# q's 32 x 32 squares: put in place by copies, or by way of memory

## The chip, the cores and the metric

The kernel runs on one core of a Trainium2 chip. Its engines, as the profile names them: PE (TensorE, matmuls), DVE (VectorE), ACT (ScalarE), POOL (GpSimd) and SP (SyncE, which here only issues DMAs). Each engine works through its own queue of instructions in order; an instruction that waits holds up what stands behind it on its engine. The metric is the time of one execution in microseconds, as the device measures it.

## The reference

Linear attention with two softmaxes, and then a mixer of two layers over tokens and two over channels, in fp32, for 8 batches, 8 heads, 576 positions and 64 numbers per head:

```python
q_s = softmax(q, axis=-1)             # over the 64 numbers of a head
k_s = softmax(k, axis=2)              # over the 576 positions
kv  = einsum('bhsd,bhse->bhde', k_s, v)
att = einsum('bhsd,bhde->bhse', q_s, kv)
x   = att.transpose(0, 2, 1, 3).reshape(8, 576, 512)
h   = maximum(x.transpose(0, 2, 1) @ w_tok1, 0) @ w_tok2
u   = x + h.transpose(0, 2, 1)
out = u + maximum(u @ w_ch1, 0) @ w_ch2
```

## The kernel before

Attention and the token mixer are cut into 32 units, numbered 0 to 31: one batch and two heads each (128 channels). A unit loads k (twice, as it is and turned), q and v, makes the two softmaxes, and then goes through five stages on PE: `stage_qT` and `stage_kv`, `stage_y` (q times w_tok1), `stage_h1`, and `stage_u` in two halves, which adds q times kv and the token mixer's second layer. The results are the columns of u. The channel mixer takes u in nine groups of 512 columns; its steps (`ch1` or `pair_a`/`pair_b`, and `ch2`) are the bulk of PE's work, and the stages of the units are spread between these steps.

Every number that goes into a matmul of a late unit (8 to 31) is split into two parts of reduced precision, a high one made by ACT (a copy that rounds, `nc.scalar.copy`) and a low one, the difference, made by DVE or POOL. `split` does both; its instructions carry the lines L134 and L135.

`stage_qT` of a late unit has to turn q: 128 positions by 128 channels, five such tiles, of which the last one holds 64 positions. DVE's transpose (L395) turns each square of 32 x 32 in its place: what it writes to the tile `cv_s` has the right numbers in each square, but a square that belongs to the partitions of group x and the columns of group y still stands at partitions y, columns x. Sixteen copies (L405), one for each pair of groups, carry the squares across partitions back into q's own tile `q_t`, which is free again once `qh` (ACT) and `ql` (POOL) have been made of it. Units 8 to 11 give every second copy to DVE and ACT; from unit 12 on DVE has 6 and ACT 10 of the 16. Then `qth` (ACT, L134) and `qtl` (DVE, L135) are made of the turned q. They are read by `stage_u` (L461), and once they are made, the load of q of the unit after next may overwrite `q_t`, of which there are two buffers (L165, issued by SP).

SP also issues the loads of `kt_t`, `k_t` and `v_t` (L173, L178, L187), the stores and loads of weights that are made on the way (L504 to L547), and, from group 3 on, the loads of the channel mixer's weights into `ring` (L585), eight buffers that PE (L642) empties in turn. The order of all instructions on each engine is fixed when the program is built, by a scheduler that places them by its own estimate of their times; the tables of steps in the code set only where a stage may begin.

The calls of `stage_qT` are in `pe_stages` (its first stage); the first late unit (8) reaches it about 167 us into the execution, the last (31) at about 642 us.

## Time and profile before

| what | value |
|---|---|
| median of 3 runs | 805.53 us (805.46 to 806.17) |
| profiled execution | 804.5 us, of which the span of its instructions is 802.7 us |
| granted TensorE clock | 1.0 |
| PE busy | 770.3 us (96%) |
| DVE busy | 654.6 us (82%) |
| ACT busy | 409.7 us (51%) |
| POOL busy | 180.2 us (22%) |
| DMA | 159.10 MB, mean 198 GB/s |

The span is what the profile's rows cover; the 1.8 us beside it lie before and after the first and the last instruction. PE's matmuls overlap each other, so that a matmul's own duration (0.39 us for 512 columns) is longer than the distance from one to the next (0.23 us). In rows of the timeline, the first number is the start in us from the span's start and the second the time that the row covers; a row of several instructions of one kind is one row with x and a count, and it may cover short waits between them; in brackets stands how long the engine was idle before it and who ended this wait. Rows with SPq or ACTq are issues of DMAs.

### The profile page before, as it was taken

To read this page: it belongs to the slowest core of one execution; us is meant where nothing else is said; L and a number is where in the kernel's file an instruction comes from. 1 tells how busy PE (TensorE), PEld (TensorE's weight loads), DVE (VectorE), ACT (ScalarE), POOL (GpSimd) and SP (SyncE) were. 2 spreads that over 40 slices of the span, in tenths; PEclk is the share of its full clock that TensorE was granted. 3 is DMA by queue.
4 is the path that set the end of the run, shared out by engine and by line. 5 is a ranking of instruction groups with operands and counts; after the bars stand their busy time and mean duration, and the time that the engine had idled before them with its cause. 6 is when DMAs were issued, how large, how long until landed. Compare 5 with 4: busy or idle time off the path is not lost.

```text
span 802.7 us, 13549 instructions
## 1 busy us (share of the span) xinstructions
PE 770.3 (96%) x4824; PEld 669.0 (83%) x4824; DVE 654.6 (82%) x1229; ACT 409.7 (51%) x952; POOL 180.2 (22%) x130
## 2 busy tenths in 40 slices
PE   3899999989999999999999999979999999999998
PEld 2688888877887888899999999869888998888886
DVE  7989998899879787987798679898998557567971
ACT  4776533465654565555564455555654534246610
POOL 0000000101211244122212121232512320446640
PEclk9999999999999999999999999999999999999999
DMA  9754842325777675575667666798956443666675
GB/s 305 218 151 150 297 148 93 110 64 186 232 240 264 220 234 162 182 256 179 188 205 228 197 179 204 252 309 246 292 166 208 142 135 110 193 195 192 194 206 197
DMA packets 124963, 159.10 MB, mean 198 GB/s; under 512 B 49376, under 2 KB 71520, under 8 KB 124896
## 3 DMA queue, kind: packets, MB, share of 16 engines
q1 hardware_dynamic: 118560, 145.91, 58.7%
q10 hardware_dynamic: 6336, 12.32, 4.1%
q8 instruction: 38, 0.62, 0.3%
q14 instruction: 29, 0.24, 0.1%
HBM read 123.60 MB, written 34.60 MB: 197 GB/s over the span
## 4 chain that ended last, share of the span: by engine, by line
PE 59%; DVE 22%; issue 7%; DMA 7%; ACT 3%; POOL 1%; SPq 0%; DVEq 0%; POOLq 0%; ACTq 0%
PE ps_o L691 16%; PE ps_h L642 10%; PE ps_h L765 7%; PE ps_o L765 6%; PE ps_h L461 6%; DMA q_t<-in_q 4%; PE ps_h L484 4%; PE ps_h L419 4%; DVE q_t L405 2%; PE ps_h L357 2%; DVE q_t L327 1%; DVE st L337 1%; DVE st L326 1%; DVE st L338 1%; PE ps_o L461 1%
## 5 line engine op out<-in xcount | busy, mean ns | idle before, releaser
L691 PE MATMUL ps_o<-h,c2h 128*128 128x512 f32 x544 | 182.4, 397 | 2.5 <-ACT h L487 2.5
L691 PEld LDWEIGHTS ps_o<-h,c2h 128*128 128x128 f32 x544 | 101.3, 188 | 22.6 <-ACT h L487 3.4
L691 PE MATMUL ps_o<-h,c2l 128*128 128x512 f32 x272 | 105.8, 392 | 0.0
L318 POOL TENSOR_TENSOR k_t<-k_t,dg 128x640 f32<-128x640 f32 x24 | 40.4, 1683 | 202.5 <-ACT dg L317 177.5
L135 POOL TENSOR_TENSOR ql<-q_t,qh 128x640 fp32r<-128x640 f32 x24 | 40.1, 1669 | 177.5 <-PE ps_o L691 101.0
L405 ACT COPY q_t<-cv_s 32x160 f32<-32x160 f32 (+1 forms) x232 | 71.8, 310 | 3.0 <-DVE cv_s L395 0.2
L642 PE MATMUL ps_h<-th,ring 128*128 128x256 f32 x384 | 71.7, 283 | 1.2 <-DVE c L673 1.2
L642 PEld LDWEIGHTS ps_h<-th,ring 128*128 128x128 f32 x384 | 59.9, 191 | 1.6 <-DVE c L673 1.6
L691 PEld LDWEIGHTS ps_o<-h,c2l 128*128 128x128 f32 x272 | 51.2, 188 | 8.7
L642 PE MATMUL ps_h<-uh,ring 128*128 128x256 f32 x288 | 54.8, 283 | 2.0 <-DVE c L669 2.0
L484 PE MATMUL ps_h<-uh,c1l 128*128 128x512 f32 x144 | 56.2, 391 | 0.0
L484 PE MATMUL ps_h<-ul,c1h 128*128 128x512 f32 x144 | 56.2, 390 | 0.0
L484 PE MATMUL ps_h<-uh,c1h 128*128 128x512 f32 x144 | 56.1, 392 | 0.0
L642 PE MATMUL ps_h<-tl,ring 128*128 128x256 f32 x192 | 54.3, 283 | 0.0
L336 ACT ACTIVATE q_t<-q_t 128x640 f32<-128x640 f32 x32 | 23.6, 738 | 51.7 <-DVE q_t L327 41.2
L642 PEld LDWEIGHTS ps_h<-uh,ring 128*128 128x128 f32 x288 | 46.0, 190 | 4.1 <-DVE c L669 2.2
L468 ACT CAST uh<-ps_h 128x320 fp32r<-128x320 f32 (+4 forms) x76 | 24.5, 335 | 46.1 <-PE ps_h L461 30.5
L326 DVE TENSOR_REDUCE st<-q_t 128x10 f32<-128x640 f32 x32 | 26.2, 817 | 24.2 <-DMA q_t<-in_q 24.1
L405 DVE COPY q_t<-cv_s 32x160 f32<-32x160 f32 (+1 forms) x152 | 37.8, 249 | 4.1 <-POOL ql L135 2.3
L642 PE MATMUL ps_h<-ul,ring 128*128 128x256 f32 x144 | 40.6, 282 | 0.0
L469 DVE TENSOR_TENSOR ul<-ps_h,uh 128x320 fp32r<-128x320 f32 (+4 forms) x76 | 27.2, 369 | 13.1 <-ACT uh L468 12.8
L642 PEld LDWEIGHTS ps_h<-tl,ring 128*128 128x128 f32 x192 | 36.8, 191 | 0.0
(321 smaller groups left out, 2110.4 us busy)
## 6 DMA issues: line engine op xcount, KB each, us to landing
ring<-w SPq DMA_DIRECT2D x210, 256.0 KB, 3.5
ring<-v SPq DMA_DIRECT2D x42, 256.0 KB, 3.0
kt_t<-in_kt SPq DMA_DIRECT2D x32, 320.0 KB, 3.7
q_t<-in_q SPq DMA_DIRECT2D x32, 320.0 KB, 3.7
v_t<-in_v SPq DMA_DIRECT2D x32, 320.0 KB, 4.3
stg_w<-in_w SPq DMA_DIRECT2D x18, 512.0 KB, 6.1
k_t<-in_k SPq DMA_DIRECT2D x24, 320.0 KB, 5.0
w<-stg SPq DMA_DIRECT2D x12, 512.0 KB, 4.2
```

The source lines that it names most:

```text
L135: lo_eng.tensor_tensor(lo, src, f32(hi), op=ALU.subtract)
L318: nc.gpsimd.tensor_tensor(kx, kx, dg.unsqueeze(1).broadcast_to([P, C1, P]), op=ALU.subtract)
L326: nc.vector.tensor_reduce(st[:, 0, :], qt, axis=AX.X, op=ALU.max)
L405: eng(qx[ys, 0:n, xs], turned[xs, 0:n, ys])
L419: nc.tensor.matmul(y[:, 0:TOK], a, w, start=(i == 0), stop=(i == len(mm) - 1))
L461: nc.tensor.matmul(t[:, 0:N], a, w, start=(i == 0), stop=(i == len(mm) - 1))
L468: nc.scalar.copy(uh, src).ins,
L469: nc.vector.tensor_tensor(ul, src, f32(uh), op=ALU.subtract).ins,
L484: nc.tensor.matmul(t, a[:, n, :], w, start=(i == 0), stop=(i == 3 * NJ - 1))
L642: nc.tensor.matmul(t[:, cols], a, b[:, n], start=(i == 0), stop=(i == 5))
L691: m = nc.tensor.matmul(o, a[:, cs], w, start=(first and i == 0), stop=(last and i == 2))
L765: nc.tensor.matmul(o, a, b, start=first and i == 0 and (n == 0 or not one), stop=last and i == 2 and (n == 1 or not one))
```

## The change

The sixteen copies are gone. The transpose writes its squares in another order within a partition (first by the group of columns, then by tile), so that the four parts of a partition, 5 x 32 numbers (640 bytes) each, can be stored by one DMA into a buffer in memory, `q8` to `q31`, one for each unit (L397, issued by SP). Four more DMAs (L399, SP too), one for each group of 32 partitions, load them to their new partitions, again 640 bytes at a time, into `q_t`. There they stand in an order of their own, and `qth` and `qtl` are made by two splits instead of one, of 512 and of 64 columns, that read `q_t` through a view with four axes and write the same `qth` and `qtl` as before.

```diff
@@ stage_qT, late units @@
-        turned = cv.tile([P, C1 * P], U32, name="cv_s").bitcast(F32).rearrange("p (c t) -> p c t", t=P)
-        nc.vector.transpose(turned, qx)
-        k = 0
-        for x in range(P // Q):
-            n = C1 if x * Q < TL else C
-            for y in range(P // Q):
-                xs, ys = slice(x * Q, (x + 1) * Q), slice(y * Q, (y + 1) * Q)
-
-                both = (nc.vector.tensor_copy, nc.scalar.copy)
-                eng = both[k % 2] if u["n"] < NE + NJ else both[k % 3 > 0]
-                k += 1
-                eng(qx[ys, 0:n, xs], turned[xs, 0:n, ys])
-        split(qth, qtl, qx.rearrange("p c t -> p (c t)")[:, 0:S], nc.vector)
+        turned = cv.tile([P, C1 * P], U32, name="cv_s").bitcast(F32).rearrange("p (y c t) -> p y c t", y=P // Q, t=Q)
+        nc.vector.transpose(turned.rearrange("p y c t -> p c y t"), qx.rearrange("p c (y t) -> p c y t", t=Q))
+        dq = dpool.tile([P // Q, P, C1 * Q], F32, name=f"q{u['n']}")
+        nc.sync.dma_start(dq.rearrange("y p f -> p y f"), turned.rearrange("p y c t -> p y (c t)"))
+        for y in range(P // Q):
+            nc.sync.dma_start(
+                qx[y * Q : (y + 1) * Q].rearrange("r c t -> r (c t)").rearrange("r (x f) -> r x f", x=P // Q),
+                dq[y].rearrange("(x r) f -> r x f", r=Q),
+            )
+        back = qx.rearrange("p c t -> p (c t)").rearrange("p (x c t) -> p c x t", x=P // Q, t=Q)
+        for hi, lo, src in ((qth[:, 0:S0], qtl[:, 0:S0], back[:, 0:C]), (qth[:, S0:S], qtl[:, S0:S], back[:, C, 0 : TL // Q, :])):
+            if len(src.shape) == 4:
+                hi, lo = (x.rearrange("p (c x t) -> p c x t", c=C, t=Q) for x in (hi, lo))
+            else:
+                hi, lo = (x.rearrange("p (x t) -> p x t", t=Q) for x in (hi, lo))
+            split(hi, lo, src, nc.vector)
```

Because the scheduler works out its order anew, other instructions move too. Line numbers behind the change are 3 higher (L461 becomes L464, L484 L487, L585 L588, L691 L694).

On **ACT**, at unit 13 (`qh` L347 is the last piece of qh, `hh` L434 is unit 13's hidden layer that `stage_u` takes, `h` L487 a step of the channel mixer). Before:

```order
L347 CAST qh<-ql 64x128
L487 ACTIVATE h_129<-ps_h 128x512
L405 COPY q_t<-cv_s 32x5x32 x5
L405 COPY q_t<-cv_s 32x4x32 x5
L434 ACTIVATE hh<-ps_h 128x256
L487 ACTIVATE h_129<-ps_h 128x512
```

And now:

```order
L347 CAST qh<-ql 64x128
L490 ACTIVATE h_129<-ps_h 128x512
L437 ACTIVATE hh<-ps_h 128x256
L134 CAST stg<-stg 128x1024
L490 ACTIVATE h_129<-ps_h 128x512
L134 CAST qth<-q_t 128x512
L134 CAST qth<-q_t 128x64
```

The ten copies that stood ahead of `hh` are gone, and `qth`, in two pieces, stands four rows behind `hh`.

On **PE**, at unit 8, the first late unit (L427 is its `stage_h1`, L461 with `qth` its `stage_u`, L484 and L691 are the channel mixer's two layers). Before:

```order
L427 MATMUL ps_h<-kvf_98,ys 128x128 x2
L461 MATMUL ps_h<-qth,kvh 128x320
L484 MATMUL ps_h<-uh_123,c1h_115 128x512
L484 MATMUL ps_h<-uh_123,c1l_116 128x512
L484 MATMUL ps_h<-ul_124,c1h_115 128x512
...
L691 MATMUL ps_o<-h_129,c2h_1258 128x512
L691 MATMUL ps_o<-h_129,c2l_1259 128x512
```

And now:

```order
L430 MATMUL ps_h<-kvf_98,ys 128x128 x2
L694 MATMUL ps_o<-h_129,c2h_1258 128x512
L694 MATMUL ps_o<-h_129,c2l_1259 128x512
...
L694 MATMUL ps_o<-h_129,c2h_1258 128x512 x4
L464 MATMUL ps_h<-qth,kvh 128x320
L487 MATMUL ps_h<-uh_123,c1h_115 128x512
L487 MATMUL ps_h<-uh_123,c1l_116 128x512
```

The twelve matmuls of L691, which came behind the twelve of L484, now stand ahead of the first one that reads `qth`.

On **SP**, where unit 17's squares come back (group 3 of the channel mixer; the names end in numbers of buffers; `q_3531` is unit 17's buffer in memory and `q_3770` unit 18's). Before:

```order
L173 DMA kt_t<-in_kt 128x640
L585 DMA ring_3167<-w_2162 128x512
L585 DMA ring_3168<-w_2162 128x512
L585 DMA ring_3169<-w_2162 128x512
L585 DMA ring_3170<-w_2162 128x512
L585 DMA ring_3171<-w_2162 128x512
```

And now:

```order
L173 DMA kt_t<-in_kt 128x640
L588 DMA ring_3103<-w_2138 128x512
L588 DMA ring_3104<-w_2138 128x512
L397 DMA q_3770<-cv_s 128x4x160
L588 DMA ring_3105<-w_2138 128x512
L588 DMA ring_3106<-w_2138 128x512
L399 DMA q_t<-q_3531 32x4x160 x4
L588 DMA ring_3107<-w_2138 128x512
```

The store of unit 18 and the four loads of unit 17 stand between loads of the ring; the ring's next load waits behind the four.

## The prediction

> **What bounds the kernel now.** I read the busy time of the engines in stretches of 50 us first, and then who made PE wait while late units are in work, 160 to 650 us.
>
> ```profile
> 150.00:200.00 50.00, 45.62 (x280) 38.07 (x279) 45.64 (x96) 27.42 (x68) 6.36 (x4) 1.00 0.42 132
> 400.00:450.00 50.00, 50.00 (x362) 46.05 (x362) 40.50 (x83) 27.30 (x71) 8.31 (x6) 1.00 0.66 206
> 500.00:550.00 50.00, 45.81 (x328) 40.80 (x327) 42.28 (x83) 25.75 (x66) 14.08 (x7) 1.00 0.84 271
> ```
>
> Each row has the stretch and its length, then the busy time of PE, PEld, DVE, ACT and POOL, the granted clock, DMA's share and GB/s. PE sets the time: 50.00 of 50 us at 400. What a faster DVE or ACT can give is what PE lacks elsewhere, in stretches in which DVE is busier than there (45.64 and 42.28 against 40.50). The waits name it:
>
> ```profile
> PE ps_o L691 <- ACT h L487: 2.5, 2, 1.3
> PE ps_h L642 <- DVE c L669: 2.0, 1, 2.0
> PE ps_h L461 <- ACT qth L134: 1.8, 1, 1.8
> PE ps_h L461 <- ACT hh L434: 1.3, 2, 0.9
> PE ps_h L642 <- DVE c L673: 1.2, 1, 1.2
> PE ps_h L461 <- DVE hl L435: 1.0, 2, 0.7
> PE ps_o L691 <- DVE h3l L679: 0.8, 1, 0.8
> PE ps_h L461 <- ACT kvh L134: 0.7, 1, 0.7
> ```
>
> Total, count and longest, in us. The eight make 11.3 us; what is left out is smaller. So the change can't give much more than 11 us, 1.4% of the time, whatever it takes off DVE and ACT.
>
> **What is removed.**
>
> ```profile
> L405 DVE COPY q_t<-cv_s x152: 205/225/1687, 169.1 to 644.0; 32x160 f32<-32x160 f32 x76, 32x128 f32<-32x128 f32 x76
> ```
> ```profile
> L405 ACT COPY q_t<-cv_s 32x160 f32<-32x160 f32 (+1 forms) x232 | 71.8, 310 | 3.0 <-DVE cv_s L395 0.2
> L405 DVE COPY q_t<-cv_s 32x160 f32<-32x160 f32 (+1 forms) x152 | 37.8, 249 | 4.1 <-POOL ql L135 2.3
> ```
>
> ACT loses 71.8 us and DVE 37.8: from unit 12 on, ten copies of 0.31 us on ACT and six of 0.25 on DVE per unit. Most of that is hidden behind PE. It counts where PE waited for something queued behind copies:
>
> ```profile
> 246.65 3.20 ACT L405 COPY q_t<-cv_s 32x160 f32<-32x160 f32 x10
> 249.88 0.38 ACT L434 ACTIVATE hh<-ps_h 128x256 fp32r<-128x256 f32 x1
> 600.41 3.20 ACT L405 COPY q_t<-cv_s 32x160 f32<-32x160 f32 x10
> 603.63 0.30 ACT L134 CAST kvh<-kvf 128x128 fp32r<-128x128 f32 x1
> ```
> ```profile
> 579.86 2.46 DVE L405 COPY q_t<-cv_s 32x160 f32<-32x160 f32 x6
> 582.35 0.69 DVE L679 SCALAR_TENSOR_TENSOR h3l<-c,h3h 128x512 fp32r<-128x512 f32 x1
> ```
> ```profile
> 535.66 1.00 DVE L405 COPY q_t<-cv_s 32x160 f32<-32x160 f32 x4
> 536.69 0.42 DVE L435 SCALAR_TENSOR_TENSOR hl<-ps_h,hh 128x256 fp32r<-128x256 f32 x1
> ```
>
> `hh`, `kvh`, `h3l` and `hl` each start right behind copies, and each is in the list of waits. Term A: 1.3 (both waits for hh) + 0.7 (kvh) + 0.8 (h3l) + 0.7 (the longer for hl) = 3.5 us gained; 0 if other work takes the copies' place, 3.5 at most.
>
> **What is added on ACT and DVE.** One split of 576 columns becomes two, of 512 and 64.
>
> ```profile
> L468 ACT CAST uh<-ps_h 128x64 fp32r<-128x64 f32 x14 | 3.0, 213 | 11.2 <-PE ps_h L461 10.1 <-DVE ul L469 1.0
> 169.97 0.62 ACT L134 CAST c2h<-cv_s 128x512 fp32r<-128x512 f32 x1
> 341.36 0.67 ACT L134 CAST qth<-q_t 128x576 fp32r<-128x576 f32 x1
> ```
>
> 0.62 + 0.21 for 0.67 us: 0.16 more on ACT per unit, and as much on DVE, 24 x 0.16 = 4 us each, a tenth of what DVE loses. It goes with the copies it replaces: hidden, and if not hidden 0.16 a unit. No row shows a read through this four-axis view or a transpose that writes in this order; I take the same times.
>
> **The way through memory.** The store and loads move 2 x 24 x 327,680 bytes = 15.7 MB on top of 159.10. Durations from the nearest rows (issue to landing, 150 to 300 us):
>
> ```profile
> w<-stg SPq DMA_DIRECT2D x12, 512.0 KB, 4.2
> q_t<-in_q SPq DMA_DIRECT2D x7, 320.0 KB, 4.4
> w<-c1h SPq DMA_DIRECT2D x6, 128.0 KB, 5.0
> v<-c2h SPq DMA_DIRECT2D x2, 128.0 KB, 3.5
> out<-part ACTq DMA_DIRECT2D x4, 256.0 KB, 2.1
> 182.66 0.47 SPq L505 DMA_DIRECT2D w<-c1h  x1
> ```
>
> A store of 320 KB: 4.2 us by the nearest. A load of 80 KB: between 2.1 and 5.0, I take 3.5, the nearer small one. Four issues are 0.5 us apart, so the last begins 1.5 after the first.
>
> In the steady part this is covered. Unit 17, as an example:
>
> ```profile
> 333.02 1.57 POOL L135 TENSOR_TENSOR ql<-q_t,qh 128x640 fp32r<-128x640 f32 x1 [3.75 <-ACT qh L134]
> 355.71 0.36 PE L461 MATMUL ps_h<-qth,kvh 128*128 128x256 f32 x1
> ```
>
> The loads may start when ql is made, 334.6; the store only needs the transpose, long done. 334.6 + 1.5 + 3.5 = 339.6, before the 341.36 at which ACT takes up qth (row above), and PE reads it 14 us later. Cost 0. On SP the four issues delay the ring's next load by 2 us; a ring buffer is refilled when PE has emptied it, and used again seven or more products later:
>
> ```profile
> ring<-w SPq DMA_DIRECT2D x210, 256.0 KB, 3.5
> L642 PE MATMUL ps_h<-th,ring x384: 278/283/386, 332.1 to 677.4; 128*128 128x256 f32 x192
> ```
>
> PE does 168 products (24 pairs of steps, seven each) in these 345 us: they take 2.05 us each, so seven are 14 us, less 3.5 for the load: 10 us of cover. Cost 0; it begins when SP is held for 10.
>
> At unit 8 it is not covered: there PE waited for `qth` already.
>
> ```profile
> 163.28 3.12 DMA whole<-cv_s
> 166.50 0.85 DVE L395 STREAM_TRANSPOSE cv_s<-q_t 128x640 f32<-128x640 f32 x1 [0.52 <-DMA whole<-cv_s]
> 171.86 0.42 PE L461 MATMUL ps_h<-qth,kvh 128*128 128x320 f32 x1 [1.84 <-ACT qth L134]
> 206.62 2.77 PE ps_o L691 x12
> ```
>
> The transpose ends at 167.35; a store of 256 KB at this place took 3.1, and with the loads (1.5 + 3.5) and the first cast (0.62) qth is there at 176.1. PE could go on at 170.0 (171.86 - 1.84) and now first does the twelve matmuls moved ahead, 2.8 us, to 172.8. It then waits 3.3 where it waited 1.8. Term B: 1.5 us lost; with 3.1 and 2.1 it is 0.1, with 4.4 and 5.0 it is 4.3.
>
> The Trainium skill (DMA: Bandwidth & Descriptors, Anatomy of one DMA) has about 2.0 us fixed plus bytes at 436 GB/s, fitted there for the other way of issuing. An estimate by it is 2.75 us for the store and 2.2 for a load, B would be about -0.1, and the forecast 1.6 lower. This trace is slower than that rule at 128 KB (3.5 and 5.0), so I stay with the rows.
>
> **Term C, the waits that are not behind a copy.** L487's 2.5 and L669's and L673's 3.2 sit in the stretches at 150 and 500. DVE loses 37.8 - 4 = 34 us of the some 480 us in which late units run, 7%, and the order is new, so these waits may vanish or come back elsewhere: -5.7 to +5.7. I take a fifth, -1.1. Ahead of L669's wait DVE took 2.02 us for ten numbers per partition, so more than the amount of work decides there:
>
> ```profile
> 526.76 2.02 DVE L338 TENSOR_SCALAR st<-st 128x10 f32<-128x10 f32 x1
> ```
>
> **Sum.** -3.5 + 1.5 - 1.1 = -3.1 us on the profiled execution's own 804.5, of which 802.7 are the span. That execution is 1.0 below the median of the runs; from the median, 805.53 - 3.1 = 802.4 us.
>
> The Trainium skill (SBUF — State Buffer, section SBUF: two separate sides) says that DVE and POOL share one pair of ports as an exclusive lock, and that a DVE instruction with two inputs from SBUF, or in a two-port mode as copies can be, waits for the whole POOL instruction. The one long copy (1687 ns against a median of 225) and the 2.02 us agree. By it A would gain at most 1.5 us more, since fewer of DVE's instructions can be caught; one copy of 152 was, so the sum leaves it out.
>
> **The rivals.** *Slower, by loads that land late.* `qth` now waits in ACT's queue for DMAs, and `qtl` in DVE's for `qth`. Behind `qth` on ACT stand the copies of u and the hidden layer `h` (L678), for which DVE's low part and then PE's L691 wait; behind the four loads on SP stands the ring. The cover at unit 17 is 341.36 - 339.6 = 1.8 us, so this decides once the last load takes over 3.5 + 1.8 = 5.3 us. For it: DMA's share is 0.84 at 500 (0.66 at 400), the slowest 128 KB row is already 5.0, and SP's order can hold the loads back. Price: at 6.0 us ACT stands 0.7 us longer in each of, say, 12 units (half of them), 8.4 us, and without cover on PE that is 805.5 - 3.1 + 8.4 = 810.8 us. Against it: median landings of 3.5 to 4.4 and PE's 14 us until it reads `qth`.
>
> The Trainium skill (DMA: Bandwidth & Descriptors, same section) holds most of the fixed time to be the wait for the write's receipt, longest when the target is memory, and that speaks for this rival, since each unit now writes memory and waits for it. Here 512 KB to memory (`w<-stg`) landed in 4.2 us and 320 KB from it (`q_t`) in 4.4: no surcharge is seen.
>
> *No change.* PE was bound before and stays so; A comes back as waits elsewhere, since freed queues only reach the next wait sooner, and B cancels the rest: 805.5 us. For it speaks 50.00 of 50 us at 400; against it that four named waits are directly behind copies.
>
> *More than forecast.* DVE's relief empties the full stretches: A 3.5, C 5.7, B 0.1 lost: 9.1 us, 796.4 us. Against it: nothing in C names a copy.
>
> **Chances.** The forecast (802.4) has 0.40, late loads 0.22, no change 0.27, more 0.11. What a measurement of this kernel can tell from no change is about 0.2%, 1.6 us. Of the forecast's 0.40 I put 0.33 beyond that bound and 0.07 within; of no change 0.02 on the fast side, 0.21 within, 0.04 on the slow side. So faster 0.33 + 0.11 + 0.02 = 0.46, same 0.28, slower 0.26. The forecast's own range is 800 to 804.5 (C from -3.5 to +1). To leave no more than 2 in 10 out, the range runs from 797, just short of the larger gain, to 810, which takes in most of the late loads.
>
> **What would show it.** Right for A: no wait of PE for `hh`, `kvh`, `h3l` or `hl` where the copies were, and DVE and ACT busy some 34 and 68 us less. Right for B: PE waits for `qth` near 173 us for about 3 us, and its store and loads land in 3.1 and 3.5 us. Right for the steady part: 50.00 of 50 us between 350 and 500 again, no wait of PE for a ring load, and ACT's wait for loads ahead of `qth` under 1 us. Wrong, on the slow side: ACT idle ahead of `qth` for DMA `q_t` by over 2 us in many units, with PE waiting for `h` right behind. Wrong, on the fast side: PE's waits at L691 and L642 gone as well. If PE's waits from 500 to 650 us are as long as before at other places, C was no gain but a matter of order.

## The result, and the profile after

The changed kernel takes 795.38 us (median of four runs, 791.96 to 796.97); the kernel before, in turn with it, 805.85 us. The ratio is 0.9863, with an interval from 0.9828 to 0.9898: 1.4% faster. A second series gave 795.09 us and a ratio of 0.9876 (0.9854 to 0.9898). The forecast was 802.4 us, with a range from 797 to 810: the direction was right, the gain three times as large, and the time lies below the range.

The profiled execution takes 796.62 us, 794.8 of them in its span. It is 1.2 us slower than the median of its runs, and the one of before was 1.0 us faster than that of its own; so the two traces differ by 7.9 us where the medians differ by 10. First the page's busy line of the changed kernel:

```profile
PE 769.0 (97%) x4824; PEld 670.9 (84%) x4824; DVE 618.1 (78%) x1101; ACT 341.9 (43%) x744; POOL 180.7 (23%) x130
```

DVE is busy 36.5 us less than before (654.6) and ACT 67.8 us less (409.7); 34 and 68 were worked out. Next PE's waits from 150 to 660 us of the changed kernel (total, count, longest), all that this view names:

```profile
PE ps_o L694 <- ACT h L490: 1.9, 3, 1.0
PE ps_o L694 <- DVE h L491: 1.0, 1, 1.0
PE ps_h L645 <- DVE c L672: 0.6, 1, 0.6
PE ps_h L464 <- DVE hl L438: 0.6, 1, 0.6
PE ps_h L464 <- DVE h L491: 0.2, 1, 0.2
```

They come to 4.3 us. The same view of before comes to 12.7: the eight rows that the prediction shows, 11.3, and 1.4 in four small ones. The waits for `hh`, `kvh`, `h3l` and `qth` are gone, and so is most of those for `c`, which stood behind no copy. The stretches show where PE gained. Before (columns as in the prediction: stretch, length, busy time of PE, PEld, DVE, ACT, POOL, clock, DMA's share, GB/s):

```profile
150.00:300.00 150.00, 144.00 (x854) 121.21 (x853) 130.25 (x264) 85.84 (x208) 30.89 (x18) 1.00 0.63 201
...
500.00:650.00 150.00, 143.13 (x1024) 128.76 (x1022) 125.30 (x248) 80.32 (x207) 40.59 (x24) 1.00 0.72 227
```

And after:

```profile
150.00:300.00 150.00, 146.78 (x866) 123.33 (x865) 124.94 (x224) 67.48 (x149) 35.83 (x22) 1.00 0.80 250
300.00:500.00 200.00, 200.00 (x1434) 181.78 (x1433) 145.82 (x274) 80.48 (x193) 40.57 (x26) 1.00 0.74 221
500.00:650.00 150.00, 148.79 (x1090) 136.47 (x1089) 119.36 (x223) 61.62 (x148) 45.12 (x26) 1.00 0.86 265
```

PE is busy 2.8 us more in the first stretch and 5.7 in the last; in between it was full and stays full. DMA's share rises from 0.72 to 0.86 in the last, without a row in which PE waits for a load.

Unit 8, where the prediction put a loss. From the timeline of the changed kernel (start, duration; in turn the transpose, the store, PE's step ahead of the twelve matmuls of L694, the loads, the first of the twelve, the two casts of `qth`, and the first weight load and matmul that read it):

```profile
169.23 0.84 DVE L395 STREAM_TRANSPOSE cv_s<-q_t 128x640 f32<-128x640 f32 x1 [0.51 <-DMA whole<-cv_s]
...
170.10 0.38 SPq L397 DMA_DIRECT2D q<-cv_s  x1
...
172.32 0.60 PE L430 MATMUL ps_h<-kvf,ys 128*128 128x128 f32 x4
172.57 1.76 SPq L399 DMA_DIRECT2D q_t<-q  x4
...
173.69 0.50 PE L694 MATMUL ps_o<-h,c2h 128*128 128x512 f32 x1 [0.76 <-ACT h L490]
...
176.11 0.77 ACT L134 CAST qth<-q_t 128x512 fp32r<-128x512 f32 x2 [2.20 <-DMA q_t<-q]
...
176.79 0.19 PEld L464 LDWEIGHTS ps_h<-qth,kvh 128*128 128x128 f32 x1 [0.49 <-ACT qth L134]
176.79 0.42 PE L464 MATMUL ps_h<-qth,kvh 128*128 128x320 f32 x1
```

From the end of the transpose (170.07) to the first cast of `qth` (176.11) pass 6.0 us, where the prediction had 8.1. The matmul that reads it starts at 176.79, without a wait of its own; only its weight load, which runs ahead, had waited 0.49. PE came there no earlier. The DMA issues of just this place (the same list as below, for 164 to 180 us; a mean of 136 GB/s) are quicker than those of all units:

```profile
q<-cv_s SPq DMA_DIRECT2D x2, 320.0 KB, 2.5
q_t<-q SPq DMA_DIRECT2D x8, 80.0 KB, 2.1
```

The list of DMA issues of the changed kernel, 150 to 660 us (count, KB each, median us to landing; a mean of 240 GB/s):

```profile
q<-cv_s SPq DMA_DIRECT2D x24, 320.0 KB, 3.2
q_t<-q SPq DMA_DIRECT2D x96, 80.0 KB, 4.1
```

Over all units the store took 3.2 us (3.1 to 4.2 were expected), the loads 4.1 (3.5, within 2.1 to 5.0). ACT's wait ahead of `qth`, in the view of waits of the changed kernel:

```profile
ACT qth L134 <- DMA q_t<-q: 11.8, 9, 2.5
```

ACT did stand for loads ahead of `qth`, nine times and up to 2.5 us, but none of PE's waits in this execution is for `qth`; in those of e17 and e18 one of 0.4 us is, at unit 8.

### The profile page after: what moved, and what is told of

Same layout as the page of the kernel before. It is cut to its first block, busy times and chain, and to the rows that moved or that the text cites. A ratio compares the mean times of both kernels' runs of the same rounds, so it can differ in the third digit from the quotient of the medians.

```text
span 794.8 us, 13455 instructions
## 1 busy us (share of the span) xinstructions
PE 769.0 (97%) x4824; PEld 670.9 (84%) x4824; DVE 618.1 (78%) x1101; ACT 341.9 (43%) x744; POOL 180.7 (23%) x130
## 2 busy tenths in 40 slices
DMA packets 151459, 174.83 MB, mean 220 GB/s; under 512 B 51297, under 2 KB 98017, under 8 KB 151393
## 4 chain that ended last, share of the span: by engine, by line
PE 70%; DVE 11%; issue 7%; DMA 7%; ACT 2%; POOL 1%; SPq 1%; DVEq 0%; POOLq 0%; ACTq 0%
PE ps_o L694 20%; PE ps_h L645 14%; PE ps_h L768 7%; PE ps_o L768 7%; PE ps_h L464 6%; PE ps_h L422 4%; PE ps_h L487 4%; PE ps_h L357 2%; DMA q_t<-in_q 2%; DMA stg<-whole 1%; PE ps_h L430 1%; PE ps_o L464 1%; PE ps_o L882 1%; DMA w<-stg 1%; DVE q_t L340 1%
## 5 line engine op out<-in xcount | busy, mean ns | idle before, releaser
L694 PE MATMUL ps_o<-h,c2h 128*128 128x512 f32 x544 | 184.2, 398 | 2.9 <-ACT h L490 1.9
L694 PEld LDWEIGHTS ps_o<-h,c2h 128*128 128x128 f32 x544 | 101.4, 188 | 23.8 <-ACT h L490 3.0
L694 PE MATMUL ps_o<-h,c2l 128*128 128x512 f32 x272 | 106.0, 393 | 0.0
L318 POOL TENSOR_TENSOR k_t<-k_t,dg 128x640 f32<-128x640 f32 x24 | 41.6, 1735 | 217.6 <-ACT dg L317 182.1
L135 POOL TENSOR_TENSOR ql<-q_t,qh 128x640 fp32r<-128x640 f32 x24 | 38.4, 1599 | 182.3 <-PE ps_o L694 104.2
L694 PEld LDWEIGHTS ps_o<-h,c2l 128*128 128x128 f32 x272 | 51.3, 188 | 8.6
L487 PE MATMUL ps_h<-uh,c1l 128*128 128x512 f32 x144 | 56.2, 390 | 0.0
L487 PE MATMUL ps_h<-ul,c1h 128*128 128x512 f32 x144 | 56.2, 390 | 0.0
L487 PE MATMUL ps_h<-uh,c1h 128*128 128x512 f32 x144 | 56.1, 392 | 0.0
L490 ACT ACTIVATE h<-ps_h 128x512 fp32r<-128x512 f32 x36 | 21.5, 598 | 49.5 <-PE ps_h L487 42.0
L135 DVE TENSOR_TENSOR qtl<-q_t,qth 128x512 fp32r<-128x512 f32 (+1 forms) x48 | 25.6, 566 | 8.1 <-ACT qth L134 7.3
```

Source lines behind the costliest of these rows:

```text
L135: lo_eng.tensor_tensor(lo, src, f32(hi), op=ALU.subtract)
L318: nc.gpsimd.tensor_tensor(kx, kx, dg.unsqueeze(1).broadcast_to([P, C1, P]), op=ALU.subtract)
L487: nc.tensor.matmul(t, a[:, n, :], w, start=(i == 0), stop=(i == 3 * NJ - 1))
L694: m = nc.tensor.matmul(o, a[:, cs], w, start=(first and i == 0), stop=(last and i == 2))
```

## The experiments

Each kernel was timed in turn with the kernel before, whose median is 804.8 to 805.9 us in all series. "Out" means that copies are left out.

| run | copies on DVE / ACT, way through memory | median us | ratio to before (interval) |
|---|---|---|---|
| e1, e2 | none, no | 796.43, 795.69 | 0.9891 (0.9862 to 0.9920), 0.9889 (0.9862 to 0.9916) |
| e3 | one copy of 16, no | 797.21 | 0.9898 (0.9872 to 0.9925) |
| e4 | all, in another order | 805.04 | 1.0003 (0.9989 to 1.0016) |
| e5 | DVE's out | 803.07 | 0.9975 (0.9953 to 0.9997) |
| e6 | ACT's out | 803.34 | 0.9965 (0.9947 to 0.9984) |
| e7 | units 8 to 23 through memory, copies behind | 799.15 | 0.9917 (0.9890 to 0.9944) |
| e8 | copies to unit 23, memory from 24 on | 798.55 | 0.9900 (0.9869 to 0.9930) |
| e9 | through memory, and copies that nobody reads | 811.97 | 1.0096 (1.0071 to 1.0121) |
| e10 | all, keep_out half a step later | 806.12 | 1.0014 (0.9996 to 1.0033) |
| e11 | through memory, one hop more | 807.98 | 1.0040 (1.0011 to 1.0069) |
| e12 | through memory, four hops more | 875.89 | 1.0897 (1.0866 to 1.0928) |
| e13 | half out on both | 801.62 | 0.9945 (0.9925 to 0.9966) |
| e14 | all on ACT | 832.94 | 1.0339 (1.0294 to 1.0385) |
| e15 | all on POOL | 803.17 | 0.9968 (0.9949 to 0.9987) |
| e16, e18 | through memory, keep_out half a step later | 793.02, 794.59 | 0.9840 (0.9809 to 0.9871), 0.9866 (0.9850 to 0.9882) |
| e17 | the changed kernel | 795.09 | 0.9876 (0.9854 to 0.9898) |

**The theory and its rivals.** Much of the gain was in waits behind which no copy stood. Three causes were possible: the work taken off the engines (of DVE, of ACT, or of both together); the new order of the instructions, which the scheduler works out anew; and the chain of q, which no longer runs through sixteen copies. A fourth question was what the way through memory costs by itself.

### All copies out

```diff
-                eng(qx[ys, 0:n, xs], turned[xs, 0:n, ys])
+                if eng is nc.scalar.copy:
+                    eng(qx[ys, 0:n, xs], turned[xs, 0:n, ys])
```

> The kernel before without DVE's share of the copies (six of 16 per unit, eight in units 8 to 11), so that these squares of the turned q keep old numbers; nothing goes through memory. DVE loses 37.8 us. If DVE's load causes the gain (the waits for c, h3l, hl and the low part of h go), this runs about 7 to 8 us below the kernel before, 797 to 799 us. If ACT's load causes it, only the waits for h3l and hl go: 1.5 us, 804 us. If the new order of the instructions causes it, the time lies anywhere between 795 and 808 us, whatever the engines lose, and waits for c appear or vanish at places where no copy was.

The second kernel has `nc.vector.tensor_copy` in that line.

> The kernel before without ACT's share of the copies (ten of 16 per unit, eight in units 8 to 11); these squares keep old numbers. ACT loses 71.8 us. If DVE's load causes the gain: the waits for hh and kvh go, 2.0 us, about 803.5 us. If ACT's load causes it: 797 to 799 us. If the order causes it: between 795 and 808 us, without relation to the amount of work taken off.

Neither edit did what its expectation says. `is` compares two newly made method objects and is never true, so both kernels lost all sixteen copies and are one and the same program. Its busy line (first of the two runs) shows it, with both engines as idle as after the change:

```profile
PE 766.0 (97%) x4824; PEld 670.0 (85%) x4824; DVE 617.3 (78%) x1077; ACT 340.5 (43%) x720; POOL 182.3 (23%) x130
```

Read as that, they answer the fourth question: without copies and without the way through memory the time is 796.43 and 795.69 us, with the way through memory 795.38 and 795.09. The intervals cover each other; what the store, the loads and the second split cost is too little to be measured, which here means under some 3 us. In the third kernel only the last copy of each unit is left:

```diff
-                eng(qx[ys, 0:n, xs], turned[xs, 0:n, ys])
+                if k == P // Q * (P // Q):
+                    eng(qx[ys, 0:n, xs], turned[xs, 0:n, ys])
```

> The kernel before with only the last of the 16 copies of each unit, so that most squares keep old numbers: the relief of the change, both engines, with no DMA added. If the way through memory costs nothing here, the time is that of the changed kernel, 795.4 us, within 2 us. If the added DMAs cost something, it is lower by that amount: at most 3.3 us (unit 8's qth) by the prediction's term B. If relief adds up, its gain is the sum of those of the kernels without DVE's and without ACT's copies; if the order decides, it is not.

797.21 us: the same gain, within its interval.

### One engine's copies out, and half of both

```diff
-                eng(qx[ys, 0:n, xs], turned[xs, 0:n, ys])
+                if eng == both[1]:
+                    eng(qx[ys, 0:n, xs], turned[xs, 0:n, ys])
```

> The kernel before without DVE's copies alone (six of 16 per unit, eight in units 8 to 11); ACT's ten stay; the squares left out keep old numbers; nothing goes through memory. DVE loses 37.8 us, ACT nothing. With all copies out the time fell by 9 us. If DVE's load is what counts (the waits for c, hl, h3l and the low part of h), 797 to 798.5 us, and hh and kvh still make PE wait. If ACT's is, 803.5 to 805 us. If each does its part, about 801 us.

The next has `both[0]` there, and the third `if y < 2:`.

> The kernel before without ACT's copies alone (ten of 16 per unit, eight in units 8 to 11); DVE's six stay; the squares left out keep old numbers. ACT loses 71.8 us, DVE nothing. If DVE's load is what counts: only the waits for hh and kvh go, 803 to 804.5 us, and c at 531 us still makes PE wait about 3 us in two pieces. If ACT's is: 797 to 798.5 us. If each does its part, about 801 us.

> The kernel before with eight of the 16 copies of each unit, three on DVE and five on ACT (four and four in units 8 to 11); the other squares keep old numbers, nothing goes through memory. DVE loses 19 us, ACT 36. If the gain follows the work taken off both engines in proportion, half of 9 us: 800 to 802 us. If it needs both engines to get below some load, it is far from half: 796 to 798 us or 804 to 806 us.

Each of the first two lies where its expectation puts the other engine's load as the cause, so neither load is the cause by itself. DVE's copies are worth 2.0 us (0.2 to 3.8), ACT's 2.8 (1.3 to 4.3), half of both 4.4 (2.7 to 6.0), and all of both 8.8 (6.4 to 11.1; by e1). Half gives half: no threshold, and no single place. That the parts of the two engines come to 4.8 and both together to 8.8 points to engines that wait for each other, but the intervals, added end to end, still overlap (1.5 to 8.1 against 6.4 to 11.1).

What relief of ACT does is seen at `hh`, which ACT makes of what PE has just written. The group's row has, behind the busy time and the mean in ns, ACT's idle time ahead of it and who ended it (160 to 650 us, 23 units). Before:

```profile
L434 ACT ACTIVATE hh<-ps_h 128x256 fp32r<-128x256 f32 x23 | 8.7, 380 | 2.8 <-DVE c L661 2.3 <-issue 0.2
```

With DVE's copies out:

```profile
L435 ACT ACTIVATE hh<-ps_h 128x256 fp32r<-128x256 f32 x23 | 8.8, 383 | 1.4 <-DVE part L712 0.9
```

With ACT's out, and after the change:

```profile
L435 ACT ACTIVATE hh<-ps_h 128x256 fp32r<-128x256 f32 x23 | 8.8, 381 | 17.2 <-PE ps_h L428 12.9 <-DVE c L662 4.3
```
```profile
L437 ACT ACTIVATE hh<-ps_h 128x256 fp32r<-128x256 f32 x23 | 8.8, 381 | 15.6 <-PE ps_h L430 15.5
```

Before, none of ACT's idle time ahead of `hh` ends by PE that is large enough to be named: when PE had written, ACT was still busy with something else. After, ACT stands ready for 15.5 us and PE ends its waiting. Whether ACT is late is a matter of its whole queue, not of the instruction directly ahead. But ACT's readiness alone is not the gain: with ACT's copies out it is there too (12.9), for 2.8 us. (The traces of these two kernels are of the fastest of ten executions each, 800.09 and 799.68 us.) The channel mixer's sums on DVE tell more (L669, and the same line under its later numbers; 500 to 650 us). Before:

```profile
L669 DVE TENSOR_TENSOR c<-ps_h,c 128x256 f32<-128x256 f32 x10 | 4.1, 405 | 1.2 <-PE ps_h L642 1.2
```

DVE's copies out, and ACT's out:

```profile
L670 DVE TENSOR_TENSOR c<-ps_h,c 128x256 f32<-128x256 f32 x10 | 4.1, 409 | 0.4 <-PE ps_h L643 0.4
```
```profile
L670 DVE TENSOR_TENSOR c<-ps_h,c 128x256 f32<-128x256 f32 x10 | 4.1, 410 | 1.7 <-PE ps_h L643 1.6
```

After:

```profile
L672 DVE TENSOR_TENSOR c<-ps_h,c 128x256 f32<-128x256 f32 x10 | 4.2, 420 | 5.5 <-PE ps_h L645 5.4
```

DVE was ready ahead of PE for 1.2 us, is ready for 5.5 after the change, but for 0.4 with its own copies out and for 1.7 with ACT's. Neither relief alone frees DVE here. A second execution of the changed kernel (e17) has 3.9, and the kernels without any copies 5.6 to 5.8. That the engines wait for each other shows in the same list: ahead of its first sum for `c` (L656) DVE stood 1.7 us for ACT before, and 4.1 with its own copies out.

### Where, and whether it is local

The changed lines in units below 24 and those of before in the others, and the other way round (`>= 24`):

```diff
+        if u["n"] < 24:
+            turned = cv.tile([P, C1 * P], U32, name="cv_s").bitcast(F32).rearrange("p (y c t) -> p y c t", y=P // Q, t=Q)
...
+        else:
+            turned = cv.tile([P, C1 * P], U32, name="cv_s").bitcast(F32).rearrange("p (c t) -> p c t", t=P)
...
```

> The change in units 8 to 23 (up to about 420 us), the copies in units 24 to 31. The traces put 3 of the 8 us gained into the stretch from 150 to 300 and none into that from 300 to 500. If the gain is local, this kernel gains 2 to 3.5 us, 802 to 803.5 us, and PE's waits from 500 to 650 us are those of the kernel before (8 to 9 us in all). If what happens late depends on the order that the early units leave behind, the late waits differ.

> The copies in units 8 to 23, the change in units 24 to 31 (from about 420 us). If the gain is local, this kernel gains 5 to 6.5 us, 799 to 800.5 us, and PE's waits from 150 to 300 us are those of the kernel before. The gains of this kernel and of the one with units 8 to 23 then add up to that of the whole change, 8 to 10 us.

The gains are 6.7 us (4.5 to 8.9) and 8.1 us (5.6 to 10.6), together 14.8, more than the 10 of the whole change: they are not local. The stretches of the one with the copies behind unit 23 (e7), and then of the one with the copies ahead of it (e8):

```profile
150.00:300.00 150.00, 146.82 (x867) 123.56 (x866) 124.14 (x223) 66.83 (x147) 37.05 (x23) 1.00 0.80 253
500.00:650.00 150.00, 145.63 (x1047) 132.17 (x1046) 126.14 (x250) 80.30 (x207) 44.98 (x26) 1.00 0.71 226
```
```profile
150.00:300.00 150.00, 144.47 (x852) 121.47 (x851) 131.03 (x266) 85.06 (x207) 30.61 (x18) 1.00 0.63 203
500.00:650.00 150.00, 149.48 (x1084) 137.36 (x1084) 118.29 (x223) 63.77 (x152) 47.64 (x27) 1.00 0.86 266
```

From 150 to 300 us each behaves as its units do: PE busy 146.82 with the way through memory (146.78 after), 144.47 with the copies (144.00 before). From 500 to 650 us e8 has all of the gain (149.48), but e7 has 2.5 us of it as well (145.63 against 143.13), with ACT as busy there as before (80.30 against 80.32). But the two kernels of the next part, with all copies and no gain, have 145.02 and 144.74 there, so little of these 2.5 us is beyond what such traces differ by. That the two gains come to more than the whole stays unexplained.

### The order by itself

The copies issued with the loops exchanged:

```diff
-        for x in range(P // Q):
-            n = C1 if x * Q < TL else C
-            for y in range(P // Q):
+        for y in range(P // Q):
+            for x in range(P // Q):
+                n = C1 if x * Q < TL else C
```

> The kernel before with its 16 copies issued in the order of the other loop (groups of partitions outside instead of groups of columns): the same number of copies on each engine, the same data, nothing relieved. If the amount of work on DVE and ACT decides, 805.5 us within 1 us. If the order of the instructions by itself moves the time by several us, this shows how much: a difference of 2 us or more either way.

The calls that the prediction's row of 2.02 us pointed to, where POOL's sum and DVE's work meet, half a step later, in the kernel before and in the changed one (the second and third expectation):

```diff
-    KEEP = (5.5, 7.5, 37, 38.5, 40, 41.5)
+    KEEP = (5.5, 7.5, 37.5, 39, 40.5, 42)
```

> The kernel before, copies and all, with the four late calls of keep_out and keep_out_sums half a step of the channel mixer later (37.5, 39, 40.5, 42 for 37, 38.5, 40, 41.5); no work is added or removed. If PE's waits for c at 531 and 535 us (3.2 us) come of POOL's sum meeting a unit's work on DVE at that place, they go or move, and the time changes by 1.5 to 4 us, down more likely than up. If they come of how much DVE and ACT have to do, the time stays at 805.5 us within 1 us.

> The changed kernel with the four late calls of keep_out and keep_out_sums half a step later. The same shift moved the kernel before by less than 2 us. If the gain between 500 and 650 us is one of work taken off, the time stays at 795.4 us within 2 us. If it is luck of the order there, it goes up by 3 us or more.

> The changed kernel with the four late calls of keep_out and keep_out_sums half a step later, in turn with the changed kernel. If the 2.4 us between the two runs seen so far are real, 792 to 794 us, with an interval of its ratio that leaves out the changed kernel's; if they are the spread of the runs, both lie at 794 to 796 us.

> The changed kernel as it is, timed in turn with the next one. 795.4 us within 1.5 us; its ratio to the kernel before 0.986 to 0.989.

Nothing moves the kernel before: 1.0003 and 1.0014, both with 1 in the interval. But moving the calls did not part what meets ahead of PE's waits for `c`. In the kernel before, these are POOL's rows there (a sum of weights, then two products of a unit):

```profile
526.37 2.39 POOL L538 TENSOR_TENSOR stg<-c2h,c2l 128x1024 f32<-128x1024 f32 x1 [8.51 <-DMA v<-stg]
528.71 1.66 POOL L318 TENSOR_TENSOR k_t<-k_t,dg 128x640 f32<-128x640 f32 x1
530.33 2.14 POOL L135 TENSOR_TENSOR ql<-q_t,qh 128x640 fp32r<-128x640 f32 x1
```

And on DVE, behind the row of 2.02 us at 526.76 that the prediction shows:

```profile
529.14 1.92 DVE L340 TENSOR_TENSOR q_t<-q_t,st 128x640 f32<-128x640 f32 x1
531.31 1.44 DVE L541 TENSOR_TENSOR stg<-stg 128x256 f32<-128x256 f32 x1
```

The shortest rows of these three lines are 0.16, 0.81 and 0.41 us. Each of the three ended 0.02 to 0.69 us behind the POOL instruction that had begun before it (at 528.76, 530.37 and 532.47), so DVE lost 4 us here, and PE's waits for `c` of 2.0 and 1.2 us end at 531.44 and 534.80, right behind. With the calls moved the same three POOL rows meet the same three lines of DVE, 1.5 us later, and PE waits 1.7 us for `c`: the meeting went along, and this run does not test what it is worth. The changed kernel seemed 2.4 us better with the calls moved, and timed beside it 0.5 us: the spread of the runs, and no version that beats it for certain. All four orders without the copies' work (e1 and e2, e3, the change, and the change with the calls moved) gain 8 to 13 us, and neither order with all of it gains any, so luck of the order does not make the 10 us; what a single wait owes to it is open.

### The work given back, or given to others

The change, and the sixteen copies too, written where the splits overwrite them:

```diff
+                both[i]((qtl, qth)[i][ys, 0 : n * Q].rearrange("p (n t) -> p n t", t=Q), turned[xs, y, 0:n, :])
```

> The changed kernel with the copies' work given back: the same 16 copies per unit, on the same engines, read the transposed squares and write them into qth (ACT's) and qtl (DVE's), which the splits overwrite; the data still go through memory and the result is whole. DVE and ACT are as busy as before the change, 655 and 410 us. If the amount of work on the two engines made the gain, it is lost: 803 to 807 us. If the copies' place in the chain of q (every unit's qth behind 16 copies of two engines, and these behind POOL's ql) made it, the time stays at 795 to 798 us.

811.97 us: all of the gain is lost, and the time is 7.7 us above that of the kernel before. Its busy line:

```profile
PE 775.8 (95%) x4824; PEld 673.1 (83%) x4824; DVE 664.3 (82%) x1253; ACT 414.7 (51%) x976; POOL 182.6 (22%) x130
```

And the two largest of PE's waits in it:

```profile
PE ps_o L703 <- ACT h L499: 3.9, 2, 2.8
PE ps_h L439 <- ACT kvf L367: 3.0, 1, 3.0
```

Nobody reads these copies, but `kvf`, which did not make PE wait before, now does for 3.0 us, and `h` for 3.9 instead of 2.5. The two additions weigh more together than apart: on engines that are relieved the way through memory costs nothing that can be measured, beside the copies 7.7 us. Some of it is this kernel's own: DVE is busy 9.7 us and ACT 5.0 us more than in the kernel before, and the copies also wait until `qth` is free of the unit before.

All on ACT, and all on POOL:

```diff
-                eng = both[k % 2] if u["n"] < NE + NJ else both[k % 3 > 0]
+                eng = nc.scalar.copy
```

> The kernel before with all 16 copies of each unit on ACT: DVE loses 37.8 us, ACT gains 152 copies of 0.31 us, 47 us; the result is whole. By the two kernels with one engine's copies out, 38 us of DVE are worth 2.7 us and 72 of ACT 2.5, so 47 more on ACT cost 1.6: 804.4 us. If the total of both engines decides, no change: 805 to 806 us. If the length of q's chain decides (16 copies of 0.31 us one after the other are 5.0 us where ten were 3.1), 807 us or more.

> The kernel before with all 16 copies of each unit on POOL: DVE and ACT lose what the change takes off them, POOL, busy 180 us, gains 384 copies of perhaps 0.3 to 0.6 us, 115 to 230 us; the result is whole, nothing goes through memory. If relief of DVE and ACT is all that counts, 795 to 798 us. If POOL's work holds up DVE's (2.02 us for ten numbers per partition was seen beside it) or q's chain grows longer, it is slower than before: 808 us or more.

ACT with 46 us more, and DVE with 31 us less, costs 27 us. PE's three largest waits in the kernel with all copies on ACT:

```profile
PE ps_h L461 <- ACT hh L434: 8.5, 9, 2.0
PE ps_o L691 <- ACT h3h L678: 6.1, 4, 1.9
PE ps_o L691 <- ACT h L487: 5.6, 4, 4.3
```

Each is for something that ACT makes, 20.2 us in the three rows. The price is far from the 1.6 us that the relief of ACT suggested: 72 us less on ACT were worth 2.8, 46 more cost 27, so it is steep on the loaded side. That each unit's chain is also 1.9 us longer (16 copies in a row for ten) is in it and was not taken apart. Nor is all of the price waiting: PE's busy time is 778.5 us for the same 4824 matmuls, 8.2 more than before (the last section says why).

All on POOL is 2.6 us better than before (1.0 to 4.1) and does not reach the change, although DVE and ACT are as free as there. Its busy line:

```profile
PE 773.1 (96%) x4824; PEld 674.3 (84%) x4824; DVE 612.7 (76%) x1077; ACT 340.2 (42%) x720; POOL 324.7 (40%) x514
```

And PE's largest wait in it:

```profile
PE ps_h L461 <- ACT qth L134: 4.4, 1, 4.4
```

POOL has 144 us more, and the first unit's `qth` comes 4.4 us late for PE: sixteen copies one after the other on one engine. There the length of q's chain is the price. The two traces say what the rest is: the spans differ by 8.4 us, PE's named waits up to 660 us by 4.3 (26.4 against 22.1), and its busy time, for the same matmuls, by 4.1 (773.1 against 769.0), of which some 2 us follow that one wait (last section). From 200 to 500 us, PE is busy all of the 300 us (298.39 before, 299.57 after the change), and from 500 to 650 it is busy 146.62 (143.13 and 148.79). So behind the first late unit the relief of the two engines brings most of the gain, although every `qth` still stands behind sixteen copies: the shorter chain of q matters at unit 8 and is not what makes the gain later.

### The way made longer

One copy from memory to memory between the store and the loads, then four:

```diff
+        for hop in range(1):
+            far = dpool.tile([P // Q, P, C1 * Q], F32, name=f"q{u['n']}_{hop}")
+            nc.sync.dma_start(far, dq)
+            dq = far
```

> The changed kernel with one more copy from memory to memory between the store and the loads of every unit, also issued by SP: the squares come back about 4 us later (store and load landed in 3.2 and 4.1 us), and 7.9 MB more are written and as many read. By the rival of late loads (ACT's cover is 1.8 us, half of the units lose the rest) ACT stands 2 us longer in 12 units: up to 820 us. If only PE's 14 us count, nothing is lost but at unit 8, where PE would wait about 3 us longer: 796 to 799 us.

> The same with four copies from memory to memory: the squares come back about 15 us later, with 31 MB more in each direction. PE's 14 us of cover are used up: each unit makes PE wait 1 to 5 us and unit 8 about 14: 815 to 850 us. If the order gives more room than the 14 us, as little as 808 us (unit 8 alone).

One hop more (3.9 us median) and the gain is gone: 807.98 us, 13 to 14 us more than the changed kernel by the ratios. ACT's wait ahead of `qth`, with one hop:

```profile
ACT qth L134 <- DMA q_t<-q: 31.3, 14, 5.6
```

And PE's three largest:

```profile
PE ps_h L468 <- ACT qth L134: 3.5, 1, 3.5
PE ps_o L698 <- ACT h L494: 3.2, 3, 1.5
PE ps_h L434 <- ACT ys L428: 3.2, 2, 2.1
```

ACT stands 31.3 us in 14 places where it was 11.8 in nine. But only 3.5 us of PE's loss is a wait for `qth`, at unit 8. The largest of the others, 2.1 us for `ys` at 536 us, comes another way (timeline of the same kernel, start and duration; the hop's issue, the issue of the load of a later unit's q, that unit's first step on DVE, `kvf` on ACT, PE):

```profile
519.83 0.49 SPq L400 DMA_DIRECT2D q<-q  x1
...
521.52 0.37 SPq L165 DMA_DIRECT2D q_t<-in_q  x1
...
527.25 0.82 DVE L326 TENSOR_REDUCE st<-q_t 128x10 f32<-128x640 f32 x1 [3.73 <-DMA q_t<-in_q]
...
532.35 0.63 ACT L367 ACTIVATE kvf<-ps_h,rs 64x64 f32<-64x64 f32 x2 [2.23 <-DVE rs L363]
...
536.25 0.71 PE L434 MATMUL ps_h<-kvf,ys 128*128 128x128 f32 x4 [2.06 <-ACT ys L428]
```

The load of q stands on SP behind the hop's issue, DVE stands 3.7 us for it, and behind DVE's row stand the sums of `kvf` and with them `ys` (a row of 1.79 us behind a POOL product, L550, is also on the way). In the whole stretch SP stands 30.1 us in 14 places until the store has landed and it may issue the hop (6.0 us in four places ahead of the loads after the change), and DVE's waits for the load of q rise from 18.3 us in 12 places to 30.0 in 16. So at the place followed the longer way costs more by what is queued behind it on SP than by ACT's standing for `qth`. Of the 11.0 us between the two spans, 4.1 are again PE's busy time (773.1 against 769.0). With four hops, at 875.89 us slower than all that was expected, PE waits for `qth` directly too, 26.5 us in four places, the longest 15.7. That the others of PE's waits go the same way as the one shown was not followed up.

## Why the prediction was right or wrong

**Term A, right.** Expected -3.5. The waits for `hh` (1.3), `kvh` (0.7) and `h3l` (0.8) are gone, those for `hl` went from 1.0 to 0.6: -3.2.

**Term B, wrong in sign.** The step that failed is the length of the way: 8.1 us (3.1 + 1.5 + 3.5) from the transpose to the first cast of `qth`, taken from rows of other places. It measured 6.0, since here the store landed in 2.5 us and a load in 2.1; e16, e17 and e18 have 6.0 to 6.1. `qth` was there 2.0 us sooner behind the transpose than the prediction had it. PE came 1.3 us later than it had: the twelve matmuls took 3.1 us instead of 2.8, and ahead of them PE stood 0.76 us for `h`, which the working left out. Together that takes away the whole 3.3 us of waiting. (In this execution the transpose and PE's step both lie almost 3 us later than in that of before; in e18's they lie where they lay, 166.39 and 169.04, and PE waits 0.4.) The wait for `qth` fell from 1.8 us to none here and to 0.4 in e17 and e18: B was -1.4 to -1.8, not +1.5. With the wait for `h` that the moved matmuls brought (0.76 to 0.81), unit 8 still gained 0.6 to 1.1 us.

**Term C, much too small.** Expected -1.1. The waits for `h` went from 2.5 to 1.9, those for `c` from 3.2 to 0.6, the four that were too small to be quoted from 1.4 to 0.2, and a new one of 1.0 (`h`, DVE) came: -3.4, the 0.76 of unit 8 included. (In e17's execution a wait for `c` of 1.6 is left, so the size differs from one execution to the next.) With A and B this is the whole difference of the two views, -3.2 - 1.8 - 3.4 = -8.4. Of the 5.3 us that the sum of -3.1 missed of it, B has 3.3 and C 2.3, and A gives 0.3 back. The step of C that failed is the fifth of 5.7 us, and the reason given for it, "nothing in C names a copy": without the copies' work the gain came in every order that was tried, half of the copies gave half of it, and with the work given back it was lost. The row of 2.02 us was read rightly, since POOL's sum held DVE up there, but it was no reason against a gain. In the changed kernel POOL's three rows of that place stand apart (they start at 520.35, 526.23 and 530.71). Whether the relief parted them or the new order was not tested; so the gain as a whole is shown to follow the work taken off, and the way of these two waits is open.

**The steady part, right.** PE is busy 200.00 of 200 us from 300 to 500, as before, with no wait for the ring.

**What ACT and DVE lose, right** (36.5 and 67.8 us), and so was the way's size (174.83 MB against 159.10).

**Late loads, right in kind, wrong in place and price.** The threshold was put at 1.8 us of ACT's cover, and loads over 5.3 us. ACT stood up to 2.5 us for loads, and PE lost nothing that can be seen by it, but for 0.4 us at unit 8 in e17 and e18; ACT has slack for it now (15.5 us ahead of `hh`), and with the copies beside it the same way cost 7.7 us (e9). One hop more, 3.9 us, is enough to lose the gain. There the price was 13 to 14 us, but at the place followed it was paid by SP's queue and the next load of q, not by `qth` on ACT, on which alone the rival's price was worked out.

**More than forecast** was the rival that came true: 796.4 us with A 3.5, C 5.7 and B 0.1 lost. Its time was right and its split was not (B gained, C gave 3.4), so that the time fits is in part luck. Its chance of 0.11 was too low; the range stopped just short of it. **No change** fell with the freed queues, which did not merely reach the next wait sooner.

**The two executions.** Ahead of 100 us, where no late unit has begun, PE's named waits are 15.7 us in the profiled execution of before, 17.8 in that of after and 16.3 in e17's, the same kernel. A sum made against one execution carries such a difference, here about as large as the 2 us between what the two traces and what the medians differ by. The profiled execution of before is also one of few with a granted clock of 1.0 throughout: over the 77 executions of it in the later series the mean is 0.996, over the nine of the changed kernel 0.9985. The difference is worth up to 1.9 us of 805, an estimate from these means; the prediction, made on that one trace, could not see it.

The Trainium skill (DMA: Bandwidth & Descriptors, Anatomy of one DMA) would have put the store at 2.75 us and a load at 2.2, an estimate by its rule of 2.0 us and bytes at 436 GB/s, which is fitted for another way of issuing. At unit 8, where term B needed them, 2.5 and 2.1 were measured, so the rule was nearer than the rows that were preferred to it; over all units, with the DMA engines busier (240 against 136 GB/s), 3.2 and 4.1.

## What to carry to other kernels

Where PE sets the time and its waits name several instructions of two helper engines, don't credit relief only to the waits right behind the removed work: look at whether the helpers' instructions that take up PE's results are waiting for PE (they have slack) or start late (here work taken off either engine helped, and work added to ACT cost steeply). Work can be moved to DMA for nothing while the engine that then waits for it, and what stands behind it on the issuing queue, have that slack; one hop of 4 us more was enough here to lose all of it. A wait of 1 to 3 us that is the difference of two paths needs transfer times from a place like its own: rows from other places put the way 2 us too long here and turned the sign; bound such a term by its sign both ways. And when a row is many times as long as others of its line, look first for a row of another engine that ends where it ends.

## What was not expected of the hardware

**POOL holds DVE up, an instruction at a time.** The rows at 526 us above are no exception. From 160 to 660 us, 45 single rows of DVE in the kernel before are over 0.2 us longer than the shortest row of their line and shape; 44 of them ended within 0.7 us behind a POOL instruction that had begun before them. They cost DVE 45 us (an estimate: what each is longer than its shortest), 38 us by the same count after the change. L327, a product with two inputs on DVE, shows it plainly. Before, from 160 to 650 us:

```profile
L327 DVE TENSOR_TENSOR q_t<-q_t,st 128x640 f32<-128x640 f32 x22 | 25.0, 1136 | 0.2
```

Fourteen of the 22 take 0.80 to 0.83 us. The other eight, 1.01 to 2.20 us, are those that began during one of POOL's products (L318 or L135), and each ended 0.67 to 0.69 us behind it. After the change the mean is 818 ns: three products of POOL began during L327, and none before it. The Trainium skill (SBUF — State Buffer, SBUF: two separate sides) has the two engines lock each other out for a whole instruction on a pair of ports; on DVE's side these rows agree. With all copies on POOL the mean is 889 ns, less than before although POOL is busy 144 us more: POOL's products met L327 three times only, and its copies are short (0.37 us on average) and hold little up.

**A long wait of PE costs more than its length.** With all copies on POOL, PE stood 4.42 us for the first `qth`, until 180.28. Its matmuls of 512 columns then started 0.43 us apart until 185 us, against 0.23 ahead of the wait, and the granted clock from 180 to 185 us is 0.50: ten of them took 2 us longer. So PE's busy time for the same 4824 matmuls differs between the kernels: 770.3 us before, 769.0 after, 773.1 with one hop more and with all copies on POOL, 778.5 with all on ACT, 787.6 with four hops. With one hop more the granted clock is 0.89 from 180 to 190 us, behind the wait of 3.5 us for `qth`, and 0.80 from 540 to 550, behind the one of 2.1 for `ys`. How long a wait must be for this is not shown: with 1.8 us for `qth` at the same place the clock stayed at 1.00 in the trace of before, and was 0.83 from 170 to 180 us in e10's.
